# Grouped-query attention over a KV cache: K read as 16 KB rows, with QK and exp re-addressed to match

## The chip, the cores and the metric

The kernel runs on one core of one Trainium2 chip. The metric is device time in microseconds (us) of one launch. TensorE does matmuls and transposes, VectorE (DVE) and ScalarE (ACT) read the matmul results from PSUM, and all loads are issued from SyncE (SP) and move from HBM to SBUF.

## The reference

```python
B, Sq, D = 32, 4, 1024
Hq, Hkv, Sk, Dh = 32, 4, 2048, 128
...
rep = Hq // Hkv
q = (x @ wq).reshape(B, Sq, Hq, Dh) transposed to (B, Hq, Sq, Dh)
k = jnp.repeat(k_cache, rep, axis=1)
v = jnp.repeat(v_cache, rep, axis=1)
scores = jnp.einsum("bhqd,bhkd->bhqk", q, k) * (Dh ** -0.5)
p = _softmax(scores, axis=-1)
o = jnp.einsum("bhqk,bhkd->bhqd", p, v)
return o transposed to (B, Sq, Hq * Dh) @ wo
```

Everything is bf16 in HBM. For each of the 32 batch entries, K and V are 2 MB each (4 heads x 2048 tokens x 128), so the two caches are 128 MB of the 151 MB that are read; wq and wo are 8 MB each.

## The kernel before, in words

**Loads.** All big loads go through nine SBUF slots of 128 partitions x 16 KB, in one fixed order on SP's queue: four parts of wq, then K of entries 0, 1, 2, then V of entry b and K of entry b+3 in turn, then four parts of wo. A load into a slot waits until the load that held it nine places earlier has been consumed. For K and for V, partition p holds tokens 16p to 16p+15 of each of the four heads: four pieces of 4 KB per partition. A part of wq is one piece of 16 KB per partition. wo has pieces of 2 KB (one row of 1024 elements per head and partition); its last part is cut into four transfers with a semaphore each.

**One entry.** Eight "kt" fills (line 240) transpose K on TensorE, eight tiles of 128 x 128 each, into one PSUM bank as bf16, and DVE (line 353) or ACT (line 355) copies the bank into `KT_sb`: fills 4, 6 and 7 go to ACT, the others to DVE. QK (line 285) is 16 matmuls of 512 columns into `ps_s`: four chunks of columns, and in each the four heads, in rows 32g to 32g+31 of the output. DVE takes the maximum of each row of `ps_s` (line 379) and makes the negative bias (line 380); ACT computes exp into `P_sb` in one instruction, with the row sum as a by-product (line 408). DVE inverts the sum and scales an identity matrix by it (lines 388 and 389: `diag`). Four "tr" fills (line 256) multiply tiles of `P_sb` with `diag`, which transposes P and normalises it; the results are copied into `PT_sb`. PV (line 267) is 64 matmuls with V's tiles as weights into `ps_o`, and DVE copies the result into `oT_sb` (line 368). After the last entry, 64 matmuls of the output projection (line 318) go into `ps_s`.

**Order.** Each engine's instructions are one list written out by the program, with semaphore waits on named events. On TensorE, iteration i holds QK(i), PV(i-1), the eight kt fills of entry i+2, the four tr fills of entry i. The kt and tr fills use four PSUM banks in turn (`ps_a`, `ps_b`, `ps_c`, `ps_o`), twelve fills per iteration; a fill waits until its bank's last fill has been copied out. On ACT, iteration i holds exp(i), the three kt copies of entry i+2, two tr copies of entry i. On DVE it holds max(i), the bias, the copy of PV(i-1), three kt copies, `rinv` and `diag`, two kt copies, two tr copies. The TensorE column order of P's tiles has to be the token order of V's partitions: tile t holds tokens 16p+t.

Of the kernel before, what the change touches and what calls it, by code (L numbers as in the profile page):

```python
# [54 lines left out]
def bass_standalone__gqa_block_cached__sampling_kernel(  # L55
# [17 lines left out]
    G = Hkv  # L73
    scale = float(Dh) ** -0.5
    NSLOT = 9
    SLOT = 8192
    NRING = 4
    KT_FILLS = 2 * G
    TR_FILLS = 4
    AHEAD = 2  # L80
    WQ_LOADS = 4
    WO_LOADS = 4
    HPL = Hq // WO_LOADS

# [5 lines left out]
    with ExitStack() as es:  # L90
        sb = lambda name, shape, dt: es.enter_context(nc.sbuf_tensor(name, shape, dt))
        slots = sb("slots", [128, NSLOT, SLOT], BF16)
        KT_sb = sb("KT_sb", [128, 2, G, Sk], BF16)
        QT_sb = sb("QT_sb", [128, B, Hq, Sq], BF16)
        oT_sb = sb("oT_sb", [128, Hq, NT], BF16)
        pp_sb = sb("pp_sb", [128, 2, Sk], BF16)
# [6 lines left out]
        P_sb = pp_sb[:, 0, :]  # L103
        PT_sb = pp_sb[:, 1, :].rearrange("p (t r) -> p t r", r=128)
        x_sb = pp_sb[:, 0, 0:D]
        xT_sb = pp_sb[:, 0, D:2 * D].rearrange("p (a b) -> p a b", b=128)
        out_sb = pp_sb[:, 1, 0:D]
# [9 lines left out]
        for n in ["x", "out"] + [f"slot{i}" for i in range(NSLOT)] + [f"wo{i}" for i in range(4)]:  # L117
            pr.sems[n] = es.enter_context(nc.semaphore(f"s_{n}"))
# [3 lines left out]
        for b in range(AHEAD + 1):  # L122
            stream.append(("k", b))
        for b in range(B):
            stream.append(("v", b))
            if b + AHEAD + 1 < B:
                stream.append(("k", b + AHEAD + 1))
# [13 lines left out]
        pr.load("sp", lambda e: e.dma_start(x_sb, x_flat[:, :]), "x", "x", 16)  # L141
        for n, l in enumerate(stream):
            kind, i = l
            waits = [freed(stream[n - NSLOT])] if n >= NSLOT else []
            s, v = f"slot{n % NSLOT}", 16 * (n // NSLOT + 1)
            if kind == "wq":
                fn = lambda e, l=l, i=i: e.dma_start(slot(l), wq_v[:, i, :])  # L147
            elif kind in "kv":
                src = (k_cache if kind == "k" else v_cache)[i].rearrange("g (p t) d -> p g (t d)", p=128)
                fn = lambda e, l=l, src=src: e.dma_start(slot(l).rearrange("p (g f) -> p g f", g=G), src)  # L150
            if kind != "wo":
                pr.load("sp", fn, l, s, v, waits)
                continue
            last = i == WO_LOADS - 1
            parts = 4 if last else 1
            per = HPL // parts
            for q in range(parts):
                fn = lambda e, l=l, i=i, q=q, per=per: e.dma_start(
                    slot(l)[:, q * per * D:(q + 1) * per * D].rearrange("p (h n) -> p h n", n=D),
                    wo_v[:, i * HPL + q * per:i * HPL + (q + 1) * per, :],  # L160
                )
                if last:
                    pr.load("sp", fn, ("wo", i, q), f"wo{q}", 16, waits)
                else:
                    pr.load("sp", fn, l, s, v, waits)
# [3 lines left out]

        jobs = [("kt", b, f) for b in range(AHEAD) for f in range(KT_FILLS)]  # L170
        for i in range(B):
            if i + AHEAD < B:
                jobs += [("kt", i + AHEAD, f) for f in range(KT_FILLS)]
            jobs += [("tr", i, f) for f in range(TR_FILLS)]
        job_index = {j: n for n, j in enumerate(jobs)}
# [6 lines left out]

        def ring_waits(job):
            n = job_index[job]
            if n < NRING:
                return [("q_evac", n)]
            w = [("evac",) + jobs[n - NRING]]
            if n % NRING == 3:
                b = job[1] - AHEAD - 1 if job[0] == "kt" else job[1] - 1
                if b >= 0:  # L190
                    w.append(("ot", b))
            return w


        pr.op("pool", lambda e: e.memset(ident[:], 0.0), [], "zero")
        pr.op("pool", lambda e: e.affine_select(
            out=ident[:], in_=ident[:], compare_op=ALU.not_equal, fill=1.0, base=0,
            pattern=[[-1, 128]], channel_multiplier=1), ["zero"], "ident")
# [33 lines left out]
        def kt_fill(b, f):  # L232
            job = ("kt", b, f)
            dst = ring_bf16[job_index[job] % NRING]
            g, half = f // 2, f % 2

            def fn(e):
                for q in range(8):
                    t = half * 8 + q
                    ins = e.transpose(  # L240
                        dst[:, q * 128:(q + 1) * 128],
                        slot(("k", b))[:, (g * NKT + t) * Dh:(g * NKT + t + 1) * Dh],
                        ident[:, :],
                    )
                return ins

            pr.op("pe", fn, [("k", b)] + ring_waits(job), job)

        def tr_fill(b, f):
            job = ("tr", b, f)  # L250
            dst = ring_f32[job_index[job] % NRING]

            def fn(e):
                for q in range(4):
                    t = f * 4 + q
                    ins = e.matmul(dst[:, q * 128:(q + 1) * 128], lhsT=P_sb[:, t * 128:(t + 1) * 128],  # L256
                                   rhs=diag[:, b % 2, :], start=True, stop=True)
                return ins

            pr.op("pe", fn, [("exp", b), ("diag", b)] + ring_waits(job), job)  # L260

        def pv(b):
            def fn(e):
                v = slot(("v", b))
                for g in range(G):
                    for t in range(NKT):
                        ins = e.matmul(  # L267
                            ps_o[:, 32 * g:32 * (g + 1)],
                            lhsT=v[:, (g * NKT + t) * Dh:(g * NKT + t + 1) * Dh],
                            rhs=PT_sb[:, t, 32 * g:32 * (g + 1)],  # L270
                            start=(t == 0),
                            stop=(t == NKT - 1),
                        )
                return ins

            w = [("v", b)] + [("evac", "tr", b, f) for f in range(TR_FILLS)]
            if b > 0:
                w.append(("ot", b - 1))
            pr.op("pe", fn, w, ("pv", b))

        def qk(i):
            def fn(e):
                for c in range(Sk // 512):
                    for g in range(G):
                        ins = e.matmul(  # L285
                            ps_s[32 * g:32 * (g + 1), c * 512:(c + 1) * 512],
                            lhsT=QT_sb[:, i, REP * g:REP * (g + 1), :],
                            rhs=KT_sb[:, i % 2, g, c * 512:(c + 1) * 512],
                            start=True,
                            stop=True,  # L290
                            tile_position=(0, 32 * g),
                        )
                return ins

            w = [("evac", "kt", i, f) for f in range(KT_FILLS)]
            w += [("q_evac", j) for j in range(NB)] if i == 0 else [("exp", i - 1)]
            pr.op("pe", fn, w, ("qk", i))
# [4 lines left out]
        for i in range(B):  # L302
            qk(i)
            if i >= 1:
                pv(i - 1)
            if i + AHEAD < B:
                for f in range(KT_FILLS):
                    kt_fill(i + AHEAD, f)
            for f in range(TR_FILLS):
                tr_fill(i, f)  # L310
        pv(B - 1)

        def oproj(i, h0, n, name):
# [15 lines left out]
        for i in range(WO_LOADS):  # L329
            last = i == WO_LOADS - 1  # L330
            parts = 4 if last else 1
            for q in range(parts):
                n = HPL // parts
                pr.op("pe", oproj(i, i * HPL + q * n, n, None),
                      [("wo", i, q) if last else ("wo", i), ("ot", B - 1), ("exp", B - 1)],
                      "oproj" if last and q == parts - 1 else None)


        def evac(job):
            eng = consumer(job)  # L340
            kind, b, f = job
            n = job_index[job]
            if kind == "kt":
                g, half = f // 2, f % 2
                src = ring_bf16[n % NRING]
                dst = KT_sb[:, b % 2, g, half * 1024:(half + 1) * 1024]
                w = [job] + ([("qk", b - 2)] if b >= 2 else [])
            else:
                src = ring_f32[n % NRING]
                dst = PT_sb[:, 4 * f:4 * f + 4, :].rearrange("p a b -> p (a b)")  # L350
                w = [job] + ([("pv", b - 1)] if b > 0 else [])
# [26 lines left out]
        for i in range(B):  # L378
# [3 lines left out]
            if i >= 1:  # L382
                ot_evac(i - 1)
# [13 lines left out]
        ot_evac(B - 1)  # L397
# [5 lines left out]
        for b in range(AHEAD):  # L403
            for f in range(KT_FILLS):
                if consumer(("kt", b, f)) == "act":
                    evac(("kt", b, f))
        for i in range(B):
            pr.op("act", lambda e, i=i: e.activation(  # L408
                P_sb, ps_s[:, :], ACT.Exp, bias=negmx[:, i:i + 1], scale=scale, accum_out=ssum[:, i:i + 1]),
# [61 lines left out]
```

## Time and profile before

| | |
|---|---|
| median of 3 runs | 389.32 us (388.3 to 391.09) |
| the profiled execution, its own time | 388.88 us |
| span from first to last instruction in it | 386.9 us |
| HBM read | 151.26 MB, 392 GB/s over the span |
| busy share of the span: PE, DVE, ACT | 77%, 63%, 51% |
| granted TensorE clock, mean | 0.938 |
| K loads: issue to landing, median | 25.0 us |

The span is shorter than the time of the run by 2.0 us, which lie before the first and after the last instruction. A busy share is a mean over the whole span, and a matmul counts as busy while it is in the pipeline, so 77% of PE isn't 77% of what PE could do. The chain of waits names what ended last; the waits table tells which engine sat idle for whom; the timeline gives the start of each group of instructions, with the idle time before it and its releaser in brackets. Landing of a load is read from the start of the first matmul that waited for it.

### The profile page before, as it was taken

How to read it: one execution, taken by the hardware profiler on the slowest of the kernel's cores; microseconds unless marked ns; L12 is line 12 of the kernel's file. 1: busy time of each engine (PE TensorE's matmuls, PEld its weight loads, DVE VectorE, ACT ScalarE, POOL GpSimd, SP SyncE). 2: the span in 40 equal slices, each digit the busy share in tenths (PEclk: the TensorE clock that was granted, in tenths of full speed). 3: DMA queues.
4: the chain of work that ended last, by engine and by line, in shares of the span. 5: the costliest groups of instructions: out<-in, count | busy, mean ns of one | idle time of the engine just before them, and what ended most of it. 6: DMA issues, size and time to landing. Idle time of an engine off the chain costs nothing.

```text
span 386.9 us, 11667 instructions
## 1 busy us (share of the span) xinstructions
PE 296.0 (77%) x5448; PEld 246.8 (64%) x5448; DVE 242.4 (63%) x390; ACT 196.6 (51%) x230; POOL 0.7 (0%) x6
## 2 busy tenths in 40 slices
PE   2877787776977977878788869877777787886596
PEld 1777576665766766767667657666666677664542
DVE  0026787775777777758777757877777577774400
ACT  1024766652655565466564635666555564664300
POOL 0000000000000000000000000000000000000000
PEclk9999999998999899889898979999999898997689
DMA  8999999999999999999999999999999999999981
GB/s 327 430 412 410 407 404 407 408 408 409 406 406 409 407 409 410 406 409 407 407 409 409 405 410 410 405 409 408 407 407 407 408 409 407 409 408 359 372 327 56
DMA packets 38912, 152.26 MB, mean 393 GB/s; under 512 B 1232, under 2 KB 1232, under 8 KB 38352
## 3 DMA queue, kind: packets, MB, share of 16 engines
q1 hardware_dynamic: 38864, 151.52, 98.5%
q8 instruction: 42, 0.69, 0.7%
q14 instruction: 6, 0.05, 0.0%
HBM read 151.26 MB, written 0.26 MB: 392 GB/s over the span
## 4 chain that ended last, share of the span: by engine, by line
DMA 87%; PE 7%; ACT 2%; DVE 2%; SPq 1%; issue 0%
DMA slots<-in_k_cache_dram 87%; PE ps_s L318 4%; DVE mx L379 1%; ACT pp_sb L408 1%; PE ps_s L285 1%; ACT KT_sb L355 1%; PE ps_a L240 1%; PE ps_o L267 0%; SPq L147 0%; PE ps_o L256 0%; PE ps_a L256 0%; PE ps_b L240 0%; SPq L150 0%; PE ps_c L256 0%; PE ps_b L256 0%
## 5 line engine op out<-in xcount | busy, mean ns | idle before, releaser
L408 ACT ACTIVATE pp_sb<-ps_s,negmx 128x2048 bf16<-128x2048 f32 x32 | 62.9, 1967 | 93.1 <-DVE negmx L380 93.1
L379 DVE TENSOR_REDUCE mx<-ps_s 128x1 f32<-128x2048 f32 x32 | 73.3, 2292 | 35.3 <-PE ps_s L285 35.3
L240 PE MATMUL ps_a<-ident,slots 128*128 128x128 bf16 x512 | 43.8, 234 | 42.2 <-DMA slots<-in_k_cache_dram 41.3
L240 PEld LDWEIGHTS ps_a<-ident,slots 128*128 128x128 bf16 x512 | 33.7, 105 | 46.1 <-DMA slots<-in_k_cache_dram 44.9
L267 PEld LDWEIGHTS ps_o<-pp_sb,slots 128*128 128x128 bf16 x2048 | 53.5, 96 | 14.6 <-issue 13.7
L267 PE MATMUL ps_o<-pp_sb,slots 128*128 128x32 bf16 x2048 | 56.7, 177 | 0.8 <-ACT pp_sb L355 0.8
L355 ACT ACTIVATE KT_sb<-ps_a 128x1024 bf16<-128x1024 bf16 x32 | 32.6, 1020 | 45.6 <-PE ps_a L240 45.6
L240 PE MATMUL ps_o<-ident,slots 128*128 128x128 bf16 x512 | 42.7, 231 | 7.8 <-DVE KT_sb L353 7.8
L353 DVE COPY KT_sb<-ps_b 128x1024 bf16<-128x1024 bf16 x64 | 43.7, 683 | 5.2 <-PE ps_b L240 5.2
L353 DVE COPY KT_sb<-ps_a 128x1024 bf16<-128x1024 bf16 x32 | 22.1, 689 | 35.0 <-PE ps_a L240 35.0
L240 PE MATMUL ps_c<-ident,slots 128*128 128x128 bf16 x512 | 43.3, 233 | 0.7 <-issue 0.7
L240 PE MATMUL ps_b<-ident,slots 128*128 128x128 bf16 x512 | 43.5, 234 | 0.0
L240 PEld LDWEIGHTS ps_o<-ident,slots 128*128 128x128 bf16 x512 | 33.8, 105 | 11.4 <-DVE KT_sb L353 11.2
L240 PEld LDWEIGHTS ps_c<-ident,slots 128*128 128x128 bf16 x512 | 34.8, 105 | 1.5 <-issue 0.9
L240 PEld LDWEIGHTS ps_b<-ident,slots 128*128 128x128 bf16 x512 | 35.2, 106 | 0.4
L285 PE MATMUL ps_s<-KT_sb,QT_sb 128*32 128x512 bf16 x512 | 34.3, 389 | 0.0
L355 ACT ACTIVATE KT_sb<-ps_c 128x1024 bf16<-128x1024 bf16 x32 | 32.7, 1021 | 1.9 <-PE ps_c L240 1.9
L355 ACT ACTIVATE KT_sb<-ps_o 128x1024 bf16<-128x1024 bf16 x32 | 32.9, 1027 | 0.0
L353 DVE CAST pp_sb<-ps_a 128x512 bf16<-128x512 f32 x32 | 22.1, 692 | 12.8 <-PE ps_a L256 12.8
L256 PE MATMUL ps_o<-diag,pp_sb 128*128 128x128 bf16 x128 | 13.2, 227 | 14.7 <-ACT KT_sb L355 14.7
L353 DVE CAST pp_sb<-ps_c 128x512 bf16<-128x512 f32 x32 | 21.9, 685 | 1.9 <-PE ps_c L256 1.6
L353 DVE COPY KT_sb<-ps_c 128x1024 bf16<-128x1024 bf16 x32 | 21.9, 684 | 1.0 <-PE ps_c L240 1.0
(46 smaller groups left out, 244.7 us busy)
## 6 DMA issues: line engine op xcount, KB each, us to landing
slots<-in_k_cache_dram SPq DMA_DIRECT2D x32, 2048.0 KB, 25.0
slots<-in_v_cache_dram SPq DMA_DIRECT2D x32, 2048.0 KB, 24.2
slots<-in_wq_dram SPq DMA_DIRECT2D x4, 2048.0 KB, 14.9
slots<-in_wo_dram SPq DMA_DIRECT2D x3, 2048.0 KB, 25.6
slots<-in_wo_dram SPq DMA_DIRECT2D x4, 512.0 KB, 12.2
pp_sb<-in_x_dram SPq DMA_DIRECT2D x1, 256.0 KB, 2.7
out_dram<-pp_sb SPq DMA_DIRECT2D x1, 256.0 KB, 2.2
```

The costliest lines, as they stand in the source:

```text
L240: ins = e.transpose(dst[:, q * 128:(q + 1) * 128], slot(("k", b))[:, (g * NKT + t) * Dh:(g * NKT + t + 1) * Dh], ident[:, :],)
L256: ins = e.matmul(dst[:, q * 128:(q + 1) * 128], lhsT=P_sb[:, t * 128:(t + 1) * 128], rhs=diag[:, b % 2, :], start=True, stop=True)
L267: ins = e.matmul(ps_o[:, 32 * g:32 * (g + 1)], lhsT=v[:, (g * NKT + t) * Dh:(g * NKT + t + 1) * Dh], rhs=PT_sb[:, t, 32 * g:32 * (g + 1)], ...
L285: ins = e.matmul(ps_s[32 * g:32 * (g + 1), c * 512:(c + 1) * 512], lhsT=QT_sb[:, i, REP * g:REP * (g + 1), :], rhs=KT_sb[:, i % 2, g, c * ...
L318: ins = e.matmul(ps_s[:, c * 512:(c + 1) * 512], lhsT=oT_sb[:, h, :], rhs=w[:, h - i * HPL, c * 512:(c + 1) * 512], start=(h == 0), stop=( ...
L353: pr.op("dve", lambda e: e.tensor_copy(dst, src), w, ("evac",) + job)
L355: pr.op("act", lambda e: e.activation(dst, src, ACT.Copy), w, ("evac",) + job)
L379: pr.op("dve", lambda e, i=i: e.tensor_reduce(mx[:, i:i + 1], ps_s[:, :], AX.X, ALU.max), [("qk", i)], ("max", i))
L408: pr.op("act", lambda e, i=i: e.activation(P_sb, ps_s[:, :], ACT.Exp, bias=negmx[:, i:i + 1], scale=scale, accum_out=ssum[:, i:i + 1]), [( ...
```

## The change

K of an entry is read as 128 rows of 16 KB: partition p holds 64 tokens of one head (head p // 32, tokens 64(p mod 32) to that plus 63), which is how the 2 MB lie in HBM, one after the other. V is read as before. Transposing tile t (t from 0 to 63) of such a slot gives 128 columns that belong to four heads, 32 columns each; so `KT_sb` is laid out as [tile][head][32], and a QK matmul of one head reads sixteen runs of 32 columns, one run in every 128. The columns of `ps_s` then stand in the order (a, t, k): token 64k + 16a + t, with a from 0 to 3, t from 0 to 15 and k from 0 to 31. PV needs P's tiles in V's order, (t, k, a). Exp makes that order: it reads `ps_s` straight through and writes `P_sb` in four passes, each with a step of four elements.

Beside this, P and PT get buffers of their own and PT a second copy; the bank of each fill is kept in a table that is filled while the program is written out; QK's waits are given for each chunk of columns; each part of wo is four transfers with a semaphore each, sixteen in all; and the memset and select that make the identity stand earlier in the text.

On SyncE, the start of the load queue and its end before, where the last columns are partitions x pieces x elements:

```order
L147 DMA slots<-in_wq_dram 128x8192 x4
L150 DMA slots<-in_k_cache_dram 128x4x2048 x3
L150 DMA slots<-in_v_cache_dram 128x4x2048
...
L150 DMA slots<-in_v_cache_dram 128x4x2048 [waits s_pe] x3
L158 DMA slots<-in_wo_dram 128x8x1024 [waits s_pe] x3
L158 DMA slots<-in_wo_dram 128x2x1024 [waits s_pe]
L158 DMA slots<-in_wo_dram 128x2x1024 x3
L166 DMA out_dram<-pp_sb 128x1024 [waits s_act,s_dve]
```

The same places with the change:

```order
L157 DMA slots<-in_wq_dram 128x8192 x4
L157 DMA slots<-in_k_cache_dram 128x8192 x3
L157 DMA slots<-in_v_cache_dram 128x4x2048
...
L157 DMA slots<-in_v_cache_dram 128x4x2048 [waits s_pe] x3
L157 DMA slots<-in_wo_dram 128x2x1024 [waits s_pe]
L157 DMA slots<-in_wo_dram 128x2x1024 x3
L157 DMA slots<-in_wo_dram 128x2x1024 [waits s_pe]
L157 DMA slots<-in_wo_dram 128x2x1024 x3
```

The order of the loads is the same; a K load has the form of a wq load, and the first three parts of wo are four transfers each.

On TensorE, the end of one iteration and the start of the next before (the four tr fills, QK, PV, the next kt fills):

```order
L256 MATMUL ps_o<-diag,pp_sb 128x128 [waits s_act]
L256 MATMUL ps_o<-diag,pp_sb 128x128 x3
L285 MATMUL ps_s<-KT_sb,QT_sb 32x512 x16
L267 MATMUL ps_o<-pp_sb,slots 128x32 [waits s_act,s_dve,s_slot0]
L267 MATMUL ps_o<-pp_sb,slots 128x32 x63
L240 MATMUL ps_a<-ident,slots 128x128 [waits s_slot1]
```

With the change:

```order
L256 MATMUL ps_o<-diag,P_sb 128x128 [waits s_act]
L256 MATMUL ps_o<-diag,P_sb 128x128 x3
L285 MATMUL ps_s<-KT_sb,QT_sb 32x512 x16
L269 MATMUL ps_o<-PT_sb,slots 128x32 [waits s_act,s_dve,s_slot0]
L269 MATMUL ps_o<-PT_sb,slots 128x32 x63
L239 MATMUL ps_a<-ident,slots 128x128 [waits s_slot1]
```

Nothing moved here: the banks and the waits are those of before, and the sixteen QK matmuls stand in one row without a wait among them.

```diff
@@ -71,16 +71,24 @@
+    KP = 128 // G
+    KTOK = Sk // KP
+    A = KTOK // NKT
...
-    KT_FILLS = 2 * G
+    KT_FILLS = KTOK // 8
     TR_FILLS = 4
     AHEAD = 2
+    LAG = 1
+    LEAD = AHEAD + LAG
+    NPT = LAG + 1
...
+    WO_PARTS = 4
+    WO_PER = HPL // WO_PARTS
...
-        KT_sb = sb("KT_sb", [128, 2, G, Sk], BF16)
+        KT_sb = sb("KT_sb", [128, 2, KTOK, G, KP], BF16)
...
-        pp_sb = sb("pp_sb", [128, 2, Sk], BF16)
+        P_buf = sb("P_sb", [128, Sk], BF16)
+        PT_buf = sb("PT_sb", [128, NPT, NKT, 128], BF16)
...
             if kind == "wq":
...
+                pr.load("sp", fetch(slot(l), wq_v[:, i, :]), l, s, v, waits)
+            elif kind == "k":
+                src = k_cache[i].rearrange("g (p t) d -> (g p) (t d)", p=KP)
+                pr.load("sp", fetch(slot(l), src), l, s, v, waits)
+            elif kind == "v":
+                src = v_cache[i].rearrange("g (p t) d -> p g (t d)", p=128)
+                pr.load("sp", fetch(slot(l).rearrange("p (g f) -> p g f", g=G), src), l, s, v, waits)
+            else:
+                for q in range(WO_PARTS):
+                    part = slot(l)[:, q * WO_PER * D:(q + 1) * WO_PER * D].rearrange("p (h n) -> p h n", n=D)
+                    h0 = i * HPL + q * WO_PER
+                    pr.load("sp", fetch(part, wo_v[:, h0:h0 + WO_PER, :]), ("wo", i, q), f"wo{i * WO_PARTS + q}", 16, waits)
...
+        bank_of = {}
+        bank_last = {n: ("q_evac", n) for n in range(NRING)}
+        turn = [0]
+
+        def take(job, evac_event, bank=None):
+            if bank is None:
+                bank = turn[0] % NRING
+                turn[0] += 1
+            bank_of[job] = bank
+            before = bank_last[bank]
+            bank_last[bank] = evac_event
+            return bank, [before]
...
         def qk(i):
-            def fn(e):
-                for c in range(Sk // 512):
+            for c in range(A):
+                def fn(e, c=c):
                     for g in range(G):
                         ins = e.matmul(
                             ps_s[32 * g:32 * (g + 1), c * 512:(c + 1) * 512],
                             lhsT=QT_sb[:, i, REP * g:REP * (g + 1), :],
-                            rhs=KT_sb[:, i % 2, g, c * 512:(c + 1) * 512],
+                            rhs=KT_sb[:, i % 2, c * NKT:(c + 1) * NKT, g, :],
...
+                w = [("evac", "kt", i, f) for f in range(2 * c, 2 * c + 2)]
+                if c == 0:
+                    w += [("q_evac", j) for j in range(NB)] if i == 0 else [("exp", i - 1)]
+                pr.op("pe", fn, w, ("qk", i) if c == A - 1 else None)
...
-                w = [job] + ([("pv", b - 1)] if b > 0 else [])
+                w = [job] + ([("pv", b - NPT)] if b >= NPT else [])
...
+        s_in = ps_s[:, :].rearrange("p (a t k) -> p a t k", a=A, k=KP)
+        p_out = P_sb.rearrange("p (t k a) -> p a t k", k=KP, a=A)
         for i in range(B):
             pr.op("act", lambda e, i=i: e.activation(
-                P_sb, ps_s[:, :], ACT.Exp, bias=negmx[:, i:i + 1], scale=scale, accum_out=ssum[:, i:i + 1]),
+                p_out, s_in, ACT.Exp, bias=negmx[:, i:i + 1], scale=scale, accum_out=ssum[:, i:i + 1]),
```

127 lines of the change are left out of this document (44 added, 83 removed).

## The prediction

> **What bounds the kernel now.** I read the page's slices and its chain first, to see whether one resource is busy throughout.
>
> ```profile
> DMA  8999999999999999999999999999999999999981
> DMA 87%; PE 7%; ACT 2%; DVE 2%; SPq 1%; issue 0%
> ```
>
> The DMA engines are full from the start to the last two slices, and 87% of the chain that ended last is loads. Next, who waits for them, in the waits table (us in total, times, longest):
>
> ```profile
> PE ps_a L240 <- DMA slots<-in_k_cache_dram: 41.3, 30, 3.4
> PEld ps_o L267 <- DMA slots<-in_v_cache_dram: 0.8, 2, 0.4
> ```
>
> In 30 of 32 iterations TensorE's first transpose waits for K, 1.4 us on average; for V it hardly waits. So an iteration lasts as long as one K and one V load. The timeline gives that period: the first and the last of six K landings in a row (start of the waiting transposes; the releaser is in the brackets).
>
> ```profile
> 103.04 0.62 PE L240 MATMUL ps_a<-ident,slots 128*128 128x128 bf16 x8 [0.18 <-DMA slots<-in_k_cache_dram]
> ...
> 154.13 0.62 PE L240 MATMUL ps_a<-ident,slots 128*128 128x128 bf16 x8 [1.80 <-DMA slots<-in_k_cache_dram]
> ```
>
> Five periods in 51.09 us: 10.22 us for two loads of equal size and form, 5.11 us for each.
>
> After the last K the chain leaves the loads. Its pieces from there (start, us, what):
>
> ```profile
> 342.52 0.62 PE ps_a L240 x8
> ...
> 348.27 1.01 PE ps_s L285 x16
> ...
> 351.81 2.07 ACT pp_sb L408 x2
> ...
> 356.37 1.86 PE ps_s L285 x15
> ...
> 360.76 2.07 ACT pp_sb L408 x2
> ...
> 363.32 0.14 issue
> ...
> 368.45 14.87 PE ps_s L318 x64
> ```
>
> From the last K's landing at 342.52 to the end at 386.9 are 44.4 us of serial work: two QK, two exp, and the output projection. The end is thus the time of the last K plus 44.4 us. The run took 388.88 us, 1.98 more than the span.
>
> **The change part by part.**
>
> *K's rows, 4 KB to 16 KB.* No K is read so in this trace, but wq is: its rows of 16 KB go into the same slots from the same queue. The last two wq landings, both waited for, and the load rates of a stretch with wq alone and of the steady state (the last column of a window is GB/s):
>
> ```profile
> 19.92 0.62 PE L215 MATMUL ps_a<-pp_sb,slots 128*128 128x128 bf16 x8 [2.38 <-DMA slots<-in_wq_dram]
> ...
> 24.82 0.62 PE L215 MATMUL ps_a<-pp_sb,slots 128*128 128x128 bf16 x8 [1.16 <-DMA slots<-in_wq_dram]
> ```
>
> ```profile
> 8.00:18.00 10.00, 8.78 (x128) 8.61 (x128) 0.00 (x0) 0.00 (x0) 0.00 (x0) 1.00 1.00 428
> 40.00:340.00 300.00, 236.63 (x4580) 200.96 (x4581) 215.46 (x347) 174.40 (x204) 0.00 (x0) 0.94 1.03 408
> 370.00:375.00 5.00, 5.00 (x24) 2.26 (x23) 0.00 (x0) 0.00 (x0) 0.00 (x0) 0.97 0.95 351
> ```
>
> By landings, 2 MB in 16 KB rows take 24.82 - 19.92 = 4.90 us against 5.11: 0.21 us less. By rates, 2.097 MB at 428 and at 408 GB/s are 4.90 and 5.14 us: 0.24 less. All 32 K loads lie ahead of the last K's landing, so the gain is 32 x 0.21 = 6.7 us, or 7.7 by the rates. I take 6.7, since PE waits for landings. The other ends: nothing, if K's rows behave otherwise than wq's; and more, from wo's 2 KB rows at 351 GB/s (5.97 us for 2 MB): if going from 2 to 4 KB, which halves the rows, takes 0.86 us off a load, a fixed cost per row would take another 0.65 off on the way to 16 KB, 20.6 us in all. wq is K's new form and size exactly; wo's stretch lies beside other work and has a DMA share of 0.95.
>
> The Trainium skill, "DMA: Bandwidth & Descriptors", section "Why small descriptors are slow (HBM only)", charges a fixed three or so cycles per packet beside one for every 32 bytes. By that a 4 KB row is 131 cycles and a quarter of a 16 KB row 128.75, 1.7% less, and the sum for 32 K loads would be 2.8 us, an estimate from that page. The 4.1% between 5.11 and 4.90 us is more than that.
>
> *Does compute follow?* The period becomes 4.90 + 5.11 = 10.01 us. One warm and one slow iteration (QK starts; K's landing in the slow one, whose eight transposes took 1.04 us instead of 0.62):
>
> ```profile
> 202.30 1.05 PE L285 MATMUL ps_s<-KT_sb,QT_sb 128*32 128x512 bf16 x16
> ...
> 206.70 1.04 PE L240 MATMUL ps_a<-ident,slots 128*128 128x128 bf16 x8 [1.66 <-DMA slots<-in_k_cache_dram]
> ...
> 213.86 1.05 PE L285 MATMUL ps_s<-KT_sb,QT_sb 128*32 128x512 bf16 x16
> ...
> 216.88 0.62 PE L240 MATMUL ps_a<-ident,slots 128*128 128x128 bf16 x8 [0.27 <-DMA slots<-in_k_cache_dram]
> ...
> 222.74 1.05 PE L285 MATMUL ps_s<-KT_sb,QT_sb 128*32 128x512 bf16 x16
> ```
>
> From QK to QK the warm one took 222.74 - 213.86 = 8.88 us with 0.27 us of wait in it. The slow one took 11.56, of which the wait is 1.66: 9.90 without it. Both lie below 10.01, the slow one closely. So the loads still end last, and what is late next is nothing until 8.88 us of work grows by 1.13.
>
> *Exp's stepped write.* Same 2048 elements in one instruction; only the destination's step is new. The nearest rows, mean ns of one:
>
> ```profile
> L408 ACT ACTIVATE pp_sb<-ps_s,negmx 128x2048 bf16<-128x2048 f32 x32 | 62.9, 1967 | 93.1 <-DVE negmx L380 93.1
> L355 ACT ACTIVATE KT_sb<-ps_a 128x1024 bf16<-128x1024 bf16 x32 | 32.6, 1020 | 45.6 <-PE ps_a L240 45.6
> L355 ACT ACTIVATE pp_sb<-ps_o 128x512 bf16<-128x512 f32 x32 | 19.1, 597 | 0.5 <-PE ps_o L256 0.5
> L363 ACT ACTIVATE QT_sb<-ps_s 128x512 bf16<-128x512 f32 x2 | 1.2, 597 | 0.6 <-PE ps_s L215 0.6
> ```
>
> The last two move the same 512 elements, one into an unbroken run, the other into `QT_sb` in runs of four elements, 256 bytes apart: 597 ns both. That scattering costs nothing; an element in every fourth place is finer still, so the lower bound is 0 and the upper one a doubled time per element: 1967 - 1020 = 947 ns for 1024 elements, 1.9 us for 2048. I take 0. A gain is excluded: no element is saved. In the steady state 1.13 us would be hidden under the load; of the tail every exp is part, so it would cost twice its excess.
>
> The Trainium skill, "SBUF — State Buffer", section "Door 1: The DMA port swizzle", says that SBUF has lines of 16 bytes, and that accesses run at full rate if at least two in a row fall into a line. A step of four bf16 is 8 bytes, two to a line: the least that the rule allows. By it exp stays at 1967 ns; no run so far shows this step.
>
> *QK's reads in runs of 32 columns.* The nearest stepped read of TensorE is the transposition of x, with a step of eight elements; its weight loads took
>
> ```profile
> L204 PEld LDWEIGHTS ps_a<-ident,pp_sb 128*128 128x128 bf16 x8 | 0.8, 164 | 3.5 <-DMA pp_sb<-in_x_dram 3.5
> L240 PEld LDWEIGHTS ps_a<-ident,slots x512: 95/98/152, 29.9 to 344.7; 128*128 128x128 bf16 x171
> ```
>
> 164 ns, against at most 152 (min, median, max) for unbroken ones, which I compare with the maximum because the first eight matmuls of line 215 also ran slow. At most 8% then: 0.08 us of QK's 1.05, and runs of 32 are broken far less. I take 0, bounds 0 and 0.16 us (two QK in the tail); a doubled QK, farther off, would still fit under the load and cost 2 us in the tail.
>
> *wo in sixteen transfers.* Nine more issues on SP, nine more waits on PE. The issues stand in a queue that is far ahead (25.0 us from issue to landing of a K load), and the projection is not held by loads:
>
> ```profile
> slots<-in_k_cache_dram SPq DMA_DIRECT2D x32, 2048.0 KB, 25.0
>   DVE oT_sb L368: 0.5, 1
> ```
>
> The second row is from the projection's own line: beside 1.7 us of issue, its PE waited for DVE only. wo and `oT_sb` both come forward with K, so that stays. Cost 0; if each of the nine waits cost as much as the 0.14 us of the chain's "issue" piece, 1.3.
>
> *The rest*, 0: the same banks in the same order; QK's four waits are for copies of an earlier iteration; PT's second copy relaxes a wait on a PV that stands ahead of the tr fills on PE anyway.
>
> Sum: 388.88 - 6.7 = 382.2 us against the profiled run's own time, which is 0.44 below the median of the three.
>
> **The rivals.**
>
> *K's rows bring less.* The 4.90 us is one undisturbed interval, with PE alone at work. K's neighbouring rows start 16 KB apart in HBM, wq's 64 KB; V's short rows stand between. Half the gain is 385.5, none 388.9. For it: the few wq loads. Against: the 428 GB/s of a stretch of 10 us. The page named above would have 386.1.
>
> *Exp becomes the bound* (the slower side). Exp stands in the loop QK, max, exp, ACT's copies, tr, next QK of 8.88 us. An excess of 1.34 us brings it to today's 10.22; beyond that the kernel is slower. At 1.9 us the period is 10.78, 0.56 above now: about 28 iterations are 15.7 us, and two exps in the tail 3.8: 408 us. For it: no row shows this step. Against: `QT_sb`'s row. A smaller excess, say 0.8 us, costs only 1.6 in the tail: 383.8.
>
> *A slow tail.* The transposes and copies after the last K took, from landing to next QK, 7.16 us when slow (206.70 to 213.86) and 5.86 when warm (216.88 to 222.74). The tail before was warm. If it is slow: 1.3 us more, 383.5.
>
> **How the numbers follow.** The forecast, 380.5 to 384.5, which holds the mild exp, the slow tail and the gain by rates (381.2), gets 0.75; half a gain, around 385.5, 0.10; no gain 0.07; exp as the bound 0.08. I predict 382.2. The range runs from 380.0 to 386.5, which takes in the half gain and leaves out some 2 in 10. About 1%, 3.9 us, is what a measurement of this kernel can tell from none; faster by more than that is a time under 385.4: the forecast and half of the half gain, 0.80; within 1% 0.12; slower 0.08.
>
> **What would show it.** In the profile after: K landings 10.0 us apart instead of 10.22; about 418 GB/s from 40 to 330 us; some 12,000 packets fewer; the last K at about 335.8 us; exp at 1967 ns, QK's sixteen at 1.05 us; the wait for K at 1.2 us an iteration; 44.4 us from the last K to the end. It would be wrong if the landings stay 10.2 apart (K's rows), or if PE stops waiting for K (exp or QK has become the bound).

## The result, and the profile after

| | before | after |
|---|---|---|
| median of 4 runs each, side by side | 389.06 us (388.3 to 391.09) | 467.54 us (466.49 to 467.87) |
| ratio | | 1.2003 (95%: 1.1953 to 1.2053) |
| the profiled execution, its own time | 388.88 us | 466.49 us |
| span | 386.9 us | 464.6 us |
| granted TensorE clock, mean | 0.938 | 0.831 |

The change made the kernel 20% slower. The forecast was 382.2 us, 380.0 to 386.5, with 0.08 for slower: it was wrong in size and in sign.

The page of the kernel after: clock, DMA share, packets, the chain by engine, exp's group and the row of the K loads.

```profile
PEclk9999778877799888878877797778888887796669
DMA  8999999999999999987988899878888988950000
DMA packets 26768, 152.26 MB, mean 328 GB/s; under 512 B 1376, under 2 KB 1376, under 8 KB 22112
...
ACT 36%; PE 31%; DVE 24%; DMA 7%; issue 2%; SPq 1%
...
L408 ACT ACTIVATE P_sb<-ps_s,negmx 128x2048 bf16<-128x2048 f32 x32 | 154.0, 4813 | 112.5 <-DVE negmx L377 112.5
...
slots<-in_k_cache_dram SPq DMA_DIRECT2D x32, 2048.0 KB, 13.7
```

Loads fell from 87% of the chain to 7%; ACT, PE and DVE share most of the rest. Exp takes 4813 ns where it took 1967: 2.85 us more for the same 2048 elements. The page counts 12,144 packets fewer than before (38,912), where some 12,000 fewer were forecast, and a K load lands 13.7 us after its issue instead of 25.0: the queue is no longer full. Two stretches of the span (start:end and length, then PE, PEld, DVE, ACT and POOL busy, the clock, the DMA share, GB/s):

```profile
40.00:180.00 140.00, 101.44 (x1716) 78.96 (x1714) 81.23 (x132) 95.54 (x77) 0.00 (x0) 0.82 1.02 417
180.00:420.00 240.00, 174.93 (x3008) 137.01 (x3008) 140.25 (x228) 164.82 (x133) 0.00 (x0) 0.83 0.84 323
```

Up to about 180 us the DMA runs at 417 GB/s (408 before) because nine slots let it run ahead of the compute. Then the slots are full, a load starts only when one comes free, and the rate falls to 323 GB/s: loads now follow compute. The waits say the same (us in total, times, longest):

```profile
PE ps_o L239 <- DVE KT_sb L350: 99.9, 30, 3.5
DVE rinv L385 <- ACT P_sb L408: 96.4, 32, 4.7
...
PE ps_a L239 <- DMA slots<-in_k_cache_dram: 2.2, 2, 1.1
```

PE's wait for K, 41.3 us before, is 2.2. In its place stand two waits in one row: DVE, whose next instruction is `rinv`, waits for exp; behind `rinv` and `diag` in DVE's list stands the copy of fill 3, and PE's eighth fill, which uses the bank `ps_o` again, waits for that copy. The chain of one iteration (start, us, what):

```profile
203.28 1.85 PE ps_s L285 x16
...
205.16 2.30 DVE mx L376
...
207.68 4.83 ACT P_sb L408 x2
...
212.99 0.61 DVE KT_sb L350
...
213.64 1.03 PE ps_o L239 x8
...
216.40 0.71 PE ps_s L285 x4
```

QK, max, exp, copy, fill, the four tr fills, the next QK: no load is in it. The timeline of PE shows two iterations in a row, from 203.21 to 216.33 and from there to 228.35, and QK of the first and the last entry (start, us, then the idle time before it in brackets):

```profile
38.04 1.05 PE L285 MATMUL ps_s<-KT_sb,QT_sb 128*32 128x512 bf16 x16
...
203.21 1.90 PE L285 MATMUL ps_s<-KT_sb,QT_sb 128*32 128x512 bf16 x16
...
213.64 1.03 PE L239 MATMUL ps_o<-ident,slots 128*128 128x128 bf16 x8 [3.33 <-DVE KT_sb L350]
...
216.33 1.22 PE L285 MATMUL ps_s<-KT_sb,QT_sb 128*32 128x512 bf16 x16
...
228.35 1.90 PE L285 MATMUL ps_s<-KT_sb,QT_sb 128*32 128x512 bf16 x16
...
431.17 1.90 PE L285 MATMUL ps_s<-KT_sb,QT_sb 128*32 128x512 bf16 x16
```

From the first QK to the last, (431.17 - 38.04) / 31 = 12.68 us an iteration, where 10.22 was the period of the loads before. This is a mean: of the two iterations shown the first, with QK at 1.90 us, lasts 13.12 us, and the second, with QK at 1.22, 12.02. QK of the last entry stood at 356.37 us in the chain of before: it starts 74.8 us later. The time from there to the end is 464.6 - 431.17 = 33.4 us against 30.5, one exp's excess. That is the whole 77.7 us of span.

It leaves two questions. Is it the step of exp's write alone, and what is it in that step? And why 12.68: the loop of 8.88 us and an excess of 2.85 make 11.73. In these rows QK takes up to 1.90 us and the eighth fill 1.03, where the warm ones of before took 1.05 and 0.62.

### The profile page after: what moved, and what is told of

It is laid out like the page before. It is cut to its first block, busy times and chain, and to the rows that moved or that the text cites. A ratio compares the mean times of both kernels' runs of the same rounds, so it can differ in the third digit from the quotient of the medians.

```text
span 464.6 us, 11674 instructions
## 1 busy us (share of the span) xinstructions
PE 330.4 (71%) x5446; PEld 256.6 (55%) x5448; DVE 241.8 (52%) x390; ACT 282.5 (61%) x230; POOL 0.7 (0%) x6
## 4 chain that ended last, share of the span: by engine, by line
ACT 36%; PE 31%; DVE 24%; DMA 7%; issue 2%; SPq 1%
ACT P_sb L408 33%; DVE mx L376 16%; PE ps_s L285 11%; DMA slots<-in_k_cache_dram 7%; PE ps_o L239 6%; DVE KT_sb L350 4%; PE ps_o L256 3%; PE ps_s L320 3%; ACT KT_sb L352 2%; PE ps_a L256 2%; PE ps_c L256 2%; PE ps_b L256 2%; DVE diag L386 2%; DVE rinv L385 1%; DVE negmx L377 1%
## 5 line engine op out<-in xcount | busy, mean ns | idle before, releaser
L408 ACT ACTIVATE P_sb<-ps_s,negmx 128x2048 bf16<-128x2048 f32 x32 | 154.0, 4813 | 112.5 <-DVE negmx L377 112.5
L269 PEld LDWEIGHTS ps_o<-PT_sb,slots 128*128 128x128 bf16 x2048 | 54.6, 98 | 23.7 <-issue 23.7
L269 PE MATMUL ps_o<-PT_sb,slots 128*128 128x32 bf16 x2048 | 57.7, 180 | 0.8 <-ACT PT_sb L352 0.8
L385 DVE RECIPROCAL rinv<-ssum 128x1 f32<-128x1 f32 x32 | 5.2, 164 | 96.4 <-ACT P_sb L408 96.4
L285 PE MATMUL ps_s<-KT_sb,QT_sb 128*32 128x512 bf16 x512 | 53.7, 563 | 0.0
L352 ACT ACTIVATE KT_sb<-ps_o 128x1024 bf16<-128x1024 bf16 x32 | 32.8, 1024 | 8.7 <-PE ps_o L239 8.2
L350 DVE CAST PT_sb<-ps_a 128x512 bf16<-128x512 f32 x32 | 22.1, 691 | 23.1 <-PE ps_a L256 23.1
L239 PEld LDWEIGHTS ps_b<-ident,slots 128*128 128x128 bf16 x512 | 30.1, 98 | 4.3 <-DVE KT_sb L350 0.6
L256 PE MATMUL ps_a<-diag,P_sb 128*128 128x128 bf16 x128 | 17.4, 279 | 12.4 <-DVE diag L386 12.4
L285 PEld LDWEIGHTS ps_s<-KT_sb,QT_sb 128*32 128x32 bf16 x512 | 13.5, 120 | 21.1 <-issue 19.5
L350 DVE CAST PT_sb<-ps_c 128x512 bf16<-128x512 f32 x32 | 22.1, 690 | 4.0 <-PE ps_c L256 3.6
## 6 DMA issues: line engine op xcount, KB each, us to landing
slots<-in_k_cache_dram SPq DMA_DIRECT2D x32, 2048.0 KB, 13.7
```

The costliest lines, as they stand in the source:

```text
L239: ins = e.transpose(dst[:, q * 128:(q + 1) * 128], slot(("k", b))[:, t * Dh:(t + 1) * Dh], ident[:, :],)
L269: ins = e.matmul(ps_o[:, 32 * g:32 * (g + 1)], lhsT=v[:, (g * NKT + t) * Dh:(g * NKT + t + 1) * Dh], rhs=PT_buf[:, b % NPT, t, 32 * g:32 * ...
L285: ins = e.matmul(ps_s[32 * g:32 * (g + 1), c * 512:(c + 1) * 512], lhsT=QT_sb[:, i, REP * g:REP * (g + 1), :], rhs=KT_sb[:, i % 2, c * NKT ...
L350: pr.op("dve", lambda e: e.tensor_copy(dst, src), w, ("evac",) + job)
L352: pr.op("act", lambda e: e.activation(dst, src, ACT.Copy), w, ("evac",) + job)
L385: pr.op("dve", lambda e, i=i: e.reciprocal(rinv[:, i:i + 1], ssum[:, i:i + 1]), [("exp", i)], ("rinv", i))
```

## The experiments

### Which part: the step without the rows, the rows without the step

The kernel after with an unbroken exp:

```diff
             pr.op("act", lambda e, i=i: e.activation(
-                p_out, s_in, ACT.Exp, bias=negmx[:, i:i + 1], scale=scale, accum_out=ssum[:, i:i + 1]),
+                P_sb, ps_s[:, :], ACT.Exp, bias=negmx[:, i:i + 1], scale=scale, accum_out=ssum[:, i:i + 1]),
```

> The kernel after, but exp writes P as an unbroken run, so P's tiles are not in V's order and PV multiplies the wrong pairs; every other part is that of the kernel after (16 KB rows, QK in runs of 32 columns, sixteen wo transfers). Theory 'step' (exp's write with a step of four is the whole loss): exp back at 1967 ns, K landings 10.0 us apart, 381 to 383 us. Rival 'other parts' (the 16 KB rows or QK's runs cost as well): QK's sixteen over 1.1 us at full clock, or landings over 10.1 us apart, and more than 385 us.

Measured: 381.61 us (381.38 to 386.83), ratio to before 0.9852 (0.9777 to 0.9928). Three of its four runs lie within 0.3 us of each other, where they were forecast; the fourth took 386.83 us and widens the interval, which still lies below 1. Its exp, two K landings five periods apart, and the stretch from 40 to 330 us:

```profile
L408 ACT ACTIVATE P_sb<-ps_s,negmx x32: 1967/1967/1969, 42.2 to 353.5; 128x2048 bf16<-128x2048 f32 x32
```

```profile
101.24 0.62 PE L239 MATMUL ps_a<-ident,slots 128*128 128x128 bf16 x8 [0.26 <-DMA slots<-in_k_cache_dram]
...
151.13 0.62 PE L239 MATMUL ps_a<-ident,slots 128*128 128x128 bf16 x8 [1.53 <-DMA slots<-in_k_cache_dram]
```

```profile
40.00:330.00 290.00, 233.20 (x4551) 197.92 (x4548) 213.95 (x345) 171.97 (x202) 0.00 (x0) 0.95 1.02 417
```

With exp back at 1967 ns (min, median, max) the loads are the bound again, at 417 GB/s, and land (151.13 - 101.24) / 5 = 9.98 us apart. Everything else of the change is in this kernel.

The kernel before, 4 KB rows and all, with the step in exp:

```diff
             pr.op("act", lambda e, i=i: e.activation(
-                P_sb, ps_s[:, :], ACT.Exp, bias=negmx[:, i:i + 1], scale=scale, accum_out=ssum[:, i:i + 1]),
+                P_sb.rearrange("p (c a) -> p a c", a=4), ps_s[:, :].rearrange("p (a c) -> p a c", a=4), ACT.Exp, bias=negmx[:, i:i + 1], scale=scale, accum_out=ssum[:, i:i + 1]),
```

> The kernel before with nothing changed but exp's write, which takes the step of four (P's tiles are then not in V's order). Theory 'step': exp at 4.8 us though K comes in 4 KB rows, and 464 to 468 us as in the kernel after, since at that period the loads wait for the compute. Rival 'together' (exp is slowed by what runs beside it in the kernel after: 16 KB packets into SBUF, or QK's reads): exp near 1967 ns and about 389 us.

Measured: 467.62 us, ratio 1.2021 (1.1969 to 1.2072), as slow as the kernel after. On its page:

```profile
L408 ACT ACTIVATE pp_sb<-ps_s,negmx 128x2048 bf16<-128x2048 f32 x32 | 154.0, 4814 | 112.3 <-DVE negmx L380 112.3
```

So the step alone makes the whole loss, and without it there is none. That the two agree to 0.1 us, with K's rows different, fits a kernel in which loads are no longer waited for.

### What in the step: lone instructions

The kernel before, with a row of lone instructions behind its end: ACT copying 512 f32 elements from PSUM to bf16 in other orders, the same on DVE, and groups of sixteen matmuls of 512 columns with stepped operands. Its total time says nothing, and each copy is one instruction that ran once. A few of the added lines:

```diff
+        pr.op("act", lambda e: e.activation(fl[:, 0:512], s512, ACT.Copy), ["out1", "out0"], "pb1")
+        pr.op("act", lambda e: e.activation(fl[:, 0:1024:2], s512, ACT.Copy), ["pb1"], "pb2")
...
+        pr.op("act", lambda e: e.activation(fl[:, 0:2048:4], s512, ACT.Copy), ["pb3"], "pb4")
+        pr.op("act", lambda e: e.activation(fl[:, 0:4096:8], s512, ACT.Copy), ["pb4"], "pb5")
...
+        pr.op("act", lambda e: e.activation(fl[:, 0:1024].rearrange("p (c f) -> p c f", f=4)[:, :, 0:2], s512, ACT.Copy), ["pb6"], "pb7")
...
+        pr.op("act", lambda e: e.activation(fl[:, 0:512].rearrange("p (c a) -> p c a", a=4), ps_s[:, :].rearrange("p (a c) -> p c a", a=4)[:, 0:128, :], ACT.Copy), ["pb8"], "pb9")
```

> The kernel before, and behind its last step a row of lone instructions, one at a time: ACT and DVE copies of 512 elements with destination steps of 1, 2, 3, 4, 8 and 16, with runs of 2 and of 4 elements, and with stepped sources; TensorE matmuls of 512 columns with stepped moving reads, stepped outputs and stepped weights. Theory 'step': 597 ns for ACT at step 1, and at step 4 about 597 + 512 x 1.39 = 1310 ns with nothing else running; if two elements to 16 bytes were enough for full rate, 597 at step 4 too and a cost only from step 8 on. Rival 'together': 597 ns at step 4. TensorE: 0.21 us per matmul where a stepped read is free, 0.43 or more where each element costs a line.

The groups of these lines. Of ACT, lines 437, 438, 440 and 441 write with a step of 1, 2, 4 and 8 elements, 443 pairs in every four places, 445 reads four PSUM banks with a step and writes unbroken. Of DVE, 456 and 458 write with a step of 1 and 4. Of PE, 421 reads its columns unbroken, 422 in runs of 32, 424 with a step of four (the number after the comma is the mean of one, in ns):

```profile
L437 ACT ACTIVATE slots<-ps_s 128x512 bf16<-128x512 f32 x1 | 0.6, 598 | 0.2 <-DVE pp_sb L398 0.2
L438 ACT ACTIVATE slots<-ps_s 128x512 bf16<-128x512 f32 x1 | 0.7, 742 | 0.0
L440 ACT ACTIVATE slots<-ps_s 128x512 bf16<-128x512 f32 x1 | 1.3, 1310 | 0.0
L441 ACT ACTIVATE slots<-ps_s 128x512 bf16<-128x512 f32 x1 | 2.5, 2456 | 0.0
L443 ACT ACTIVATE slots<-ps_s 128x512 bf16<-128x512 f32 x1 | 0.6, 597 | 0.0
L445 ACT ACTIVATE slots<-ps_s 128x512 bf16<-128x512 f32 x1 | 0.6, 597 | 0.0
...
L456 DVE CAST slots<-ps_s 128x512 bf16<-128x512 f32 x1 | 0.7, 692 | 66.1 <-ACT slots L455 66.1
L458 DVE CAST slots<-ps_s 128x512 bf16<-128x512 f32 x1 | 1.3, 1289 | 0.0
...
L421 PE MATMUL ps_b<-slots,ident 128*128 128x512 bf16 x16 | 3.6, 379 | 0.0
L422 PE MATMUL ps_b<-slots,ident 128*128 128x512 bf16 x16 | 3.6, 379 | 0.0
L424 PE MATMUL ps_b<-slots,ident 128*128 128x512 bf16 x16 | 7.4, 629 | 0.0
```

It is the write, on DVE as on ACT. ACT's reading side is free: a stepped read from PSUM takes the same 597 ns. That doesn't hold for DVE: in the same run its copy of 1024 bf16 elements from PSUM took 692 ns unbroken (line 460) and 1224 with a stepped read and an unbroken write (line 461), where ACT took 1024 ns for either (lines 454 and 455). Pairs of elements are free too. For TensorE, runs of 32 columns cost nothing, lone columns with a step of four double the time.

Two readings were left. Either the number of 16-byte lines touched decides ("line": pairs farther apart would slow down), or a 2-byte element that stands alone in its aligned four bytes does ("word": pairs stay fast wherever they stand, and slow down when they start at an odd place). A second row of ACT copies tells them apart, on the kernel before again:

```diff
+        pr.op("act", lambda e: e.activation(fl[:, 0:4096].rearrange("p (c f) -> p c f", f=16)[:, :, 0:2], s512, ACT.Copy), ["pb2"], "pb3")
...
+        pr.op("act", lambda e: e.activation(fl[:, 1:1025].rearrange("p (c f) -> p c f", f=4)[:, :, 0:2], s512, ACT.Copy), ["pb4"], "pb5")
...
+        pr.op("act", lambda e: e.activation(f2[:, 0:4096:8], s512, ACT.Copy), ["pb6"], "pb7")
...
+        pr.op("act", lambda e: e.activation(fl[:, 0:2048].rearrange("p (c a) -> p a c", a=4), ps_s[:, :].rearrange("p (a c) -> p a c", a=4), ACT.Copy), ["pb10"], "pb11")
+        pr.op("act", lambda e: e.activation(fl[:, 0:2048].rearrange("p (c a) -> p c a", a=4), ps_s[:, :].rearrange("p (a c) -> p c a", a=4), ACT.Copy), ["pb11"], "pb12")
```

> The kernel before with a second row of lone ACT copies behind it, 512 elements unless said: aligned pairs in every eighth and sixteenth place, pairs that start on an odd element, two 4-byte elements in every 16 bytes, one 4-byte element in 32 bytes, a stepped write from an SBUF source, and 2048 elements with stepped write, stepped read and neither. Theory 'word' (slow are 2-byte elements that stand alone in their aligned 4 bytes): aligned pairs at about 600 to 620 ns wherever they lie, pairs on odd starts as slow as a step of two, 742 ns. Rival 'line' (4.46 ns for every 16 bytes that are touched and not filled, as steps 2, 3, 4 and 8 all gave): pairs in every eighth place 256 x 4.46 + 171 = 1310 ns, pairs on odd starts 742 too. Both: a stepped write of 2048 elements 4.7 us, a stepped read of them as fast as none, 1.87 us.

Its groups: 426 writes pairs in every sixteen places, 428 pairs in every four from an odd place on, 430 f32 elements with a step of eight, 432 a step of four again but read from SBUF; 434 and 435 are 2048 elements with a stepped write and with a stepped read.

```profile
L434 ACT ACTIVATE slots<-ps_s 128x2048 bf16<-128x2048 f32 x1 | 4.7, 4694 | 0.0
L435 ACT ACTIVATE slots<-ps_s 128x2048 bf16<-128x2048 f32 x1 | 1.9, 1877 | 0.0
...
L432 ACT ACTIVATE slots<-slots 128x512 bf16<-128x512 bf16 x1 | 1.3, 1335 | 0.0
L430 ACT ACTIVATE slots<-ps_s 128x512 f32<-128x512 f32 x1 | 1.1, 1085 | 0.0
L428 ACT ACTIVATE slots<-ps_s 128x512 bf16<-128x512 f32 x1 | 0.7, 738 | 0.0
L426 ACT ACTIVATE slots<-ps_s 128x512 bf16<-128x512 f32 x1 | 0.6, 628 | 0.0
```

"Word" holds: pairs in every eight places took 620 ns (line 425), where "line" forecast 1310, and pairs in every sixteen 628; pairs in every four places, 597 ns in the first row, go to 738 when they start at an odd place. "Line" falls as it was put, but lines still count (last section). From SBUF the stepped write is as slow, 1335 ns against 629 unbroken (line 433). Line 434 has the exp's write without the exp, and shows its loss: 4694 against 1877 ns for the same elements in the same order of places, stepped in the read instead (435).

### How much excess is free

The kernel before with a step of two, to have a smaller excess in the same place:

```diff
-                P_sb, ps_s[:, :], ACT.Exp, bias=negmx[:, i:i + 1], scale=scale, accum_out=ssum[:, i:i + 1]),
+                P_sb.rearrange("p (c a) -> p a c", a=2), ps_s[:, :].rearrange("p (a c) -> p a c", a=2), ACT.Exp, bias=negmx[:, i:i + 1], scale=scale, accum_out=ssum[:, i:i + 1]),
```

> The kernel before with exp's write in two passes with a step of two elements (P's tiles are then not in V's order). From the lone copies, 742 - 597 = 145 ns per 512 elements: exp at 1967 + 580 = 2550 ns. Theory 'slack' (the loop of 8.88 us grows to 9.46, below the 10.22 of the loads, so only the tail's two exps are paid): 390 us, within 1% of before. Rival 'every exp counts': 32 x 0.58 = 18.6 us, 407 us.

Measured: 391.16 us, ratio 1.0065 (1.0043 to 1.0086).

```profile
L408 ACT ACTIVATE pp_sb<-ps_s,negmx x32: 2523/2552/2569, 42.5 to 361.0; 128x2048 bf16<-128x2048 f32 x32
```

```profile
PE ps_a L240 <- DMA slots<-in_k_cache_dram: 39.6, 29, 3.3
```

Exp takes 0.585 us more, 32 times, 18.7 us in all, and PE goes on waiting for K. Loads set the period as before; of the exps only the two behind the last K show, 2.58 us each in the chain instead of 2.07. The run is 2.2 us longer than before (391.16 against 388.98); the other 1.2 us I did not follow, beyond a piece of 0.52 us before the output projection that was 0.14 before. So an excess of 0.585 us is hidden and one of 2.85 is not, as the prediction's threshold of 1.34 us would have it; where between the two the threshold lies was not measured.

### Why 12.68 and not 11.73

The first idea was the order on DVE: the copies of fills 3 and 5 stand behind `rinv`, so PE's eighth fill waits for exp. This kernel is the one after with those copies ahead of `rinv` and `diag`:

```diff
-            for job in fills[:3]:
+            for job in fills:
                 if consumer(job) == "dve":
                     evac(job)
...
-            for job in fills[3:]:
-                if consumer(job) == "dve":
-                    evac(job)
```

> The kernel after with DVE's two late K copies moved ahead of rinv and diag, so that TensorE's eighth transposition no longer waits for DVE behind exp. Theory 'loop through DVE' (of the 2.46 us by which the period grew, 2.85 come from exp, and TensorE's idle time before the eighth fill, 3.3 us, then runs it at half clock): the loop goes through ACT's copies again, 8.88 + 2.85 = 11.7 us, and the time is 434 to 440 us. Rival (the order on DVE does not matter, exp alone sets the loop): 464 to 468 us.

Measured: 458.89 us, ratio 1.1796 (1.1753 to 1.1839), 8.65 us less than the kernel after. The wait did move, and the 434 to 440 us did not come. Three views of it: the waits, QK's matmuls (min, median, max), the timeline of PE.

```profile
PE ps_a L256 <- ACT KT_sb L352: 73.9, 30, 2.7
```

```profile
L285 PE MATMUL ps_s<-KT_sb,QT_sb x512: 378/634/635, 38.2 to 425.6; 128*32 128x512 bf16 x171
```

```profile
199.59 1.90 PE L285 MATMUL ps_s<-KT_sb,QT_sb 128*32 128x512 bf16 x16
...
209.79 0.40 PE L256 MATMUL ps_a<-diag,P_sb 128*128 128x128 bf16 x4 [2.20 <-ACT KT_sb L352]
...
212.15 1.90 PE L285 MATMUL ps_s<-KT_sb,QT_sb 128*32 128x512 bf16 x16
```

PE now waits for ACT's copies, which stand behind exp. The period is 212.15 - 199.59 = 12.56 us: 8.88 + 2.85 and the 0.85 us that QK takes longer than its 1.05. The median matmul of QK takes 634 ns instead of 379. The suspicion was then that TensorE is slowed by its own idle time in front of the tr fills. The test gives it more work: 36 matmuls of the identity with itself in each iteration, into a bank that the next fill overwrites, on top of the kernel just shown.

```diff
                     kt_fill(i + AHEAD, f)
+                def filler(e):
+                    for _ in range(36):
+                        ins = e.matmul(ring_f32[1][:, 0:128], lhsT=ident[:, :], rhs=ident[:, :], start=True, stop=True)
+                    return ins
+                pr.op("pe", filler, [("evac", "kt", i + AHEAD, 5)])
```

> The kernel with DVE's copies first, and behind the eighth transposition of each iteration 36 matmuls that multiply the identity with itself into a free PSUM bank, about 2.0 us at full clock, so that TensorE is busy while exp's excess passes. Its results are overwritten. Theory 'idle TensorE' (the 0.85 us by which the loop exceeds 8.88 + 2.85 is QK at half clock, 1.90 instead of 1.05 us, after an idle TensorE): QK back at 1.05 us, the period at 11.7 to 11.8 us, 434 to 438 us, though there is more work. Rival (QK is slow for another reason, its runs of 32 columns or DVE's and ACT's reads of PSUM beside it): QK stays at 1.90, 459 us or more.

Measured: 429.63 us, ratio 1.104 (1.0955 to 1.1125), 29 us less than without the added work, and some 4 us less than the forecast's lower end. Its clock row and its timeline of PE:

```profile
PEclk9989999999999999999999999999999999997679
```

```profile
199.57 1.05 PE L285 MATMUL ps_s<-KT_sb,QT_sb 128*32 128x512 bf16 x16
...
206.40 2.18 PE L312 MATMUL ps_b<-ident 128*128 128x128 bf16 x36
...
211.10 1.05 PE L285 MATMUL ps_s<-KT_sb,QT_sb 128*32 128x512 bf16 x16
```

The granted clock is 0.976 over the span (0.817 without the filler), QK is back at 1.05 us, and the period is 11.53 us, 0.2 us below 8.88 + 2.85, which stays unexplained. In the iteration shown the granted clock is 1.00, against 0.77 in the one without the filler. Exp is as slow as ever here. So the loss of the reordered kernel has two parts: exp's excess, which by itself leaves it at about 430, and about 29 us more from TensorE running at half speed after the idle time that the excess opens. The filler was run on the reordered kernel only; that it would bring as much in the order of the kernel after wasn't tried. The iterations of the kernel after show the same effect, though: apart from the first and the last, the eight whose QK took 1.05 to 1.22 us lasted 11.85 to 12.03 us, close to 8.88 + 2.85, and the others, with QK at 1.90, 12.69 to 13.12.

The Trainium skill, "TensorE: Matmul & The Clock Gate", section "Why this matters for your kernels", asks for no idle gaps over about 3 us between bursts of matmuls. The trace agrees with the kind of effect, not with the size: in the reordered kernel the longest wait in the loop was 2.7 us and the one shown 2.20, and QK behind it ran at half speed. The slowing does not begin right behind the wait: of the four tr fills between the 2.20 us and QK, three took 0.39 or 0.40 us, as they do with the filler, and the last 0.61.

### The same order of P by a stepped read

Since ACT's stepped read from PSUM is free, exp can make V's order from that side: it reads `ps_s` with a step of 512 columns and writes `P_sb` straight through.

```diff
-        s_in = ps_s[:, :].rearrange("p (a t k) -> p a t k", a=A, k=KP)
-        p_out = P_sb.rearrange("p (t k a) -> p a t k", k=KP, a=A)
+        s_in = ps_s[:, :].rearrange("p (a c) -> p c a", a=A)
+        p_out = P_sb.rearrange("p (c a) -> p c a", a=A)
```

> The kernel after with the reordering moved to the other side of exp: it reads the scores from PSUM with the innermost step of 512 elements (four passes become the innermost dimension) and writes P as one unbroken run, in V's order. Theory 'write side only' (the lone copies showed 597 ns for such a read and 1310 for the stepped write): exp at 1967 ns, K landings 10.0 us apart, 381 to 383 us. Rival 'reordering costs wherever it stands' (2048 elements over four banks, with DVE's maximum and TensorE on other banks): exp over 3 us, and more than 390 us.

Measured: 381.82 us (381.3 to 381.87), ratio 0.9818 (0.98 to 0.9835): 1.8% faster than the kernel before, and P is in V's order here, so that PV multiplies the right pairs.

```profile
L408 ACT ACTIVATE P_sb<-ps_s,negmx x32: 1967/1967/1969, 41.9 to 353.6; 128x2048 bf16<-128x2048 f32 x32
```

```profile
111.11 0.62 PE L239 MATMUL ps_a<-ident,slots 128*128 128x128 bf16 x8 [1.10 <-DMA slots<-in_k_cache_dram]
...
151.01 0.62 PE L239 MATMUL ps_a<-ident,slots 128*128 128x128 bf16 x8 [1.59 <-DMA slots<-in_k_cache_dram]
...
335.45 0.62 PE L239 MATMUL ps_a<-ident,slots 128*128 128x128 bf16 x8 [1.57 <-DMA slots<-in_k_cache_dram]
```

Exp takes 1967 ns, the first two landings are four periods of 9.98 us apart, and the last K is there at 335.45 us instead of 342.52. This is the gain that the prediction counted.

## Why the prediction was wrong

**K's rows: right.** The term was 32 x 0.21 = 6.7 us, with landings 10.01 us apart, 418 GB/s and the last K at 335.8. With exp unbroken they are 9.98 apart at 417 GB/s; with the stepped read, whose last K lands 342.52 - 335.45 = 7.07 us earlier, 4.87 us are left for a K load if V's stays at 5.11. The kernel that has this part and not the slow write ran in 381.8 us, where 382.2 was forecast. The estimate of 2.8 us, made from the Trainium skill's "DMA: Bandwidth & Descriptors", was too small by more than half.

**Compute follows the loads: right as far as it went.** The step of two shows an excess of 0.585 us hidden as long as loads land. That the loop of before has 1.34 us to spare fits this and the loss at 2.85 us; the runs say no more than that the limit lies between the two.

**Exp's stepped write, taken as 0 with bounds 0 and 1.9 us: the step that failed.** It costs 4812 - 1967 = 2.85 us, half as much again as the upper bound. The choice went by the row of `QT_sb`, 597 ns for runs of four elements and for an unbroken run alike, as "nearest". It wasn't near. A run of four bf16 elements is two whole 4-byte words; the new write leaves each element alone in its word, and that is what costs: 597 ns for pairs, 1310 for single elements at the same step of four. None of the rows that I set beside it writes a 2-byte element alone, and the bound from above, a doubled time per element, had no such row behind it either: the time per element went from 0.83 to 2.22 ns. With no row near, exp as the bound should have had far more than 0.08.

The Trainium skill's rule that was set beside it, "SBUF — State Buffer", section "Door 1: The DMA port swizzle" (full rate if two accesses in a row fall into a 16-byte line), had nothing to do with the sum but agreed with the 0. The runs contradict it for this write: a step of four puts two elements into every line, and took 1310 ns against 598; a step of two puts four, and took 742.

**The rival "exp becomes the bound": the right mechanism, too small.** Its sum with 2.85 us in place of 1.9 is a period of 11.73 us, 28 x 1.51 + 2 x 2.85 = 48 us, and 437 us in all. The rest to 467.5, some 30 us, is for the most part an effect that no rival held for the loop: while PE waits for exp, its clock falls, and QK, which is on the loop, takes 1.90 us. The profile of before had that effect in the slow iterations that the prediction quoted (transposes of 1.04 us for 0.62); I counted it in the tail, for 1.3 us, and not in a loop bound by compute, where most iterations pay it.

**QK's runs of 32, wo's sixteen transfers, the rest, each taken as 0: right.** Lone matmuls take 3.6 us for sixteen either way. With exp unbroken the span is 7.1 us shorter than before and the last K lands 335.58 instead of 342.52, 6.9 earlier; that leaves a few tenths of a microsecond at most for what these parts could have cost.

## What to carry to other kernels

Before a stepped write of 2-byte elements is put on a loop, ask whether each element keeps a neighbour in its four bytes; if not, make the order on ACT's reading side, or in aligned pairs; on DVE a stepped read had a price too. A row of the profile bounds an unseen operation only if it has the property that is new: here it was single elements, and the row had runs. And where compute becomes the bound, count TensorE's own slowing in it: the idle time that a wait opens can be paid a second time in the matmuls behind it.

## What the runs showed of the hardware

**One price per 16-byte line, and two kinds of line.** ACT's unbroken copies of 512 and of 2048 f32 elements in the second probe, 598 and 1877 ns (lines 424 and 436), are 0.83 ns per element and about 171 ns beside them. Without the 171, most ACT copies of 512 elements fit two numbers; a step of sixteen, 2347 ns or 4.25 ns per line, lies 5% below. They are worked out from the rows above, and are a fit, not a mechanism that was seen:

| write | elements per 16 bytes | ns per element | ns per 16-byte line that is written |
|---|---|---|---|
| unbroken | 8 | 0.83 | 6.7 |
| step 2 | 4 | 1.12 | 4.46 |
| pairs from an odd place | 4 | 1.11 | 4.43 |
| step 4 | 2 | 2.22 | 4.45 |
| step 8 | 1 | 4.46 | 4.46 |
| pairs in every sixteen | 2 in one line, none in the next | 0.89 | 1.79 |
| f32, step 8 | 1 in one line, none in the next | 1.79 | 1.79 |

A line in which 2-byte elements stand alone costs about 4.45 ns, one of whole 4-byte words about 1.8, and the engine's own 0.83 ns per element is the floor. DVE's step of four, 1289 ns against 692, is of the same size. Why a lone element costs this much was not seen.

**The clock can be bought back with useless work.** 36 matmuls of 2.2 us per iteration made a kernel 29 us faster (458.9 to 429.6): QK took 1.90 us behind the idle time and 1.05 where they filled it.

**What stays open.** The 12.68 us of the kernel after are a mean of slow iterations and of fast ones, in which QK ran at or near full speed; in the reordered kernel QK took 1.58 us or more in every iteration after the first, and the mean is (424.30 - 38.24) / 31 = 12.45 us. Why TensorE gets its speed back in every third or fourth iteration of the one kernel and not in the other was not found out.
